# A fused Nystrom attention and SiLU feed-forward kernel: another start for batch 0, exp(C) written straight, a last block in halves, and a new plan

## The chip, the core and the metric

The kernel runs on one core of a Trainium2 chip. The metric is the time of one execution on the device, in microseconds (us). The kernel before takes 275.34 us, the median of three runs (274.78 to 275.83). One further execution was recorded by the profiler; its own time and span are in the table below.

The core's engines appear in the profile under these names: PE (TensorE, matrix products; PEld is its weight load, which overlaps), DVE (VectorE), ACT (ScalarE), POOL (GpSimd) and SP (SyncE, which here only issues DMAs). POOL issues the loads from memory, SP the stores.

## The reference

There are 8 batches of 8 heads, 576 positions and a head size of 64. q, k and v are float32. Each batch goes through an attention with 32 landmarks, and the result through a feed-forward layer of 512 to 2048 to 512 with SiLU between.

```python
q_lm = q.reshape(B, H, 32, 18, D).mean(axis=3)      # landmarks: means of 18 positions
k_lm = k.reshape(B, H, 32, 18, D).mean(axis=3)
A  = softmax(q    @ k_lm.T / 8)                     # 576 x 32
Bm = softmax(q_lm @ k_lm.T / 8)                     # 32 x 32
C  = softmax(q_lm @ k.T    / 8)                     # 32 x 576
Z  = Bm.T / (norm1(Bm) * norminf(Bm) + 1e-6)
for _ in range(6):
    Z = 2 * Z - Z @ Bm @ Z                          # pseudo-inverse of Bm
x = A @ Z @ C @ v                                   # heads side by side: (8*576) x 512
out = silu(x @ w_in) @ w_out                        # 512 -> 2048 -> 512, float32
```

## The kernel before, in words

**What each batch does.** k and q of a batch are loaded by two DMAs each, one to partitions 0 to 63 and one to 64 to 127, and are cast from float32 to bf16 by the loading DMA (`load`). v is loaded by one DMA to 96 partitions, also cast. `landmarks` sums groups of 18 positions: for batches 0 to 2 by products with the identity on PE, for later batches by a tree of additions on POOL in the buffers `treek` and `treeq`; the results `lm` are transposed into `lmT` by DVE. `turn` transposes k and q into `kT` and `qT` on DVE. `scores_b`, `scores_c` and `scores_a` multiply the landmarks with each other, with k and with q.

`exps_c` makes exp(B) (for batch 0 into `be`) and exp(C), which it writes as `pc`; `exps_a` makes exp(A) as `ea`, after `top_a` has subtracted the row maximum in `s_sb`. `norm_b` normalises B to `bm` and prepares the first iterate, `gd` or `gx`. `values` transposes `pc` by products with the identity, copies the result to `pt`, and multiplies it with v. The six steps of the pseudo-inverse are `steps` for batches 0 and 1 (products in `gd` and `tc`, copied by ACT and DVE) and `steps_x` for the later ones. `z_of` gives `zt`, which is Z C v of the eight heads. `weights_a` divides `ea` by its row sums (`asum`, `arec`) and transposes it into `at`.

**The feed-forward layer.** It is never computed from x. `mix` multiplies `zt` with w_in, which gives `m`, 32 landmarks of each head by 2048. `layer1` multiplies `at` with `m` and takes SiLU on ACT into `g`. `layer2` multiplies `g` of a pair of batches with w_out, in blocks of 128 rows by 512 columns: 16 products of 512 columns into `o`, a copy by ACT into `ost`, two stores by SP. There are 36 such blocks.

For batch 0, `mix` makes four parts of 512 columns: part 0 goes to the accumulator `h0`, parts 1 to 3 to `o0` and `o1`. Layer 1 of batch 0 can start once part 0 has been copied to `m` by DVE (first half) and ACT (second half).

**What sets the order.** No loop sets the order of the work. Each operation is added to a planner (`_Plan.add`) with its engine, an estimated duration, the buffers that it reads and writes, and a priority. `_Plan.schedule` then runs a list schedule: at each point it takes, for the engine that is free first, the ready operation with the lowest priority value. It models eight loads in flight on POOL, and the blocks of 256 instructions in which PE's program is fetched. The instructions are issued in the order of planned start times; each engine runs its own in that order, and waits at run time by semaphores for what it reads. `SEQ` is the order in which the stages are added, and `SHIFT` a table of corrections to single priorities.

**Products of zeros.** In gaps of PE, the planner puts products of a buffer of zeros, written to `o1` and read by nobody. Before, they are of 512 columns, go into gaps over 1.0 us, and end for good at the first operation with `hold`, batch 0's first product for the scores of A. There are 14: 10 at the start, 2 behind the landmarks of k and 2 behind those of q.

**The start of the program.** POOL issues the two loads of k of batch 0, then the two of q, then makes the identity matrix, then v, the four loads of w_in, k and q of batch 1, and the four loads of w_out with small operations between.

All products go through the helper `mm` (line 231 in the profile), so the profile tells them apart by their tiles.

Of the kernel before, what the change touches and what calls it, by code (L numbers as in the profile page):

```python
# [16 lines left out]
SEQ = ['E0', 'M0', 'S1', 'L0', 'X1', 'K2', 'M1', 'E2', 'L1', 'M2', 'E3', 'L2', 'M3', 'E4', 'L3', 'M4', 'E5', 'L4', 'E6', 'M5', 'L5', 'M6', 'E7', 'L6', 'M7', 'L7']  # L17
# [3 lines left out]
SHIFT = {'DVE gx t 3': 2, 'DVE brec bsum 2': -1, 'DVE qT qn 3': -0.25, 'PE o zt 0': -0.25, 'ACT xp h 0': -2, 'PE t btd 3': 0.75, 'DVE bm t 2': 2, 'POOL treek 3': 0.25, 'DVE rn n 3': 0.5, 'DVE crec csum 1': -0.5, 'POOL ea arec 1': 1, 'DVE amax s 3': -0.5, 'DVE lmT lm 3': -2, 'PE t gx 3': 2, 'DVE crec csum 3': -0.25, 'DVE pt h 2': -0.25}  # L21

XM = 0.15
# [7 lines left out]
class _Plan:  # L31
# [43 lines left out]
    def schedule(self):  # L75
# [4 lines left out]
        dma_free = 0.0  # L80
# [21 lines left out]
        while left:  # L102
# [27 lines left out]
            if n.tab is not None:  # L130
                if n.tab != tab:
                    occ += 1.3
                tab = n.tab
            if e == "PE" and self.filler is not None:
                from_ = max(free[e], released)
                gap = start - from_
                if n.hold:
                    self.filler = None
                elif gap > 1.0:
                    k = int((gap - 0.3) / 0.35)  # L140
                    for x in range(k):
                        f = _Node()
                        f.start, f.fn = from_ + 0.35 * x, self.filler
# [57 lines left out]
def kernel(  # L201
# [43 lines left out]
    tree = {t: sb(f"tree{t}", [128, 2, 9, D], FP) for t in "qk"}  # L245
# [61 lines left out]
    def emit_consts():  # L307
        V.memset(zero, 0.0)
# [8 lines left out]
        V.memset(tiny, 0.0)  # L317
# [13 lines left out]
    def constants():  # L331
        P.add("DVE", 1.5, emit_consts, w=["mask", "xp", "zero", "tiny", "t0"], prio=-10)
        P.add("POOL", 0.5, emit_ident, w=["s0"], prio=-5)
        P.add("DVE", 0.7, emit_cast, r=["s0"], w=["ident", "two"], prio=-9)
        P.filler = lambda: mm(o_ps[1], zero[:, 0:128], zero)
# [24 lines left out]
    def load(t, src, b):  # L360
        if t == "v":
            def f():
                G.dma_start(  # L363
                    out=nat[t][b % 2][0:96].rearrange("p h j d -> p h (j d)"),
                    in_=src[b].rearrange("h (p j) d -> p h (j d)", j=6))
            P.add("POOL", 0.7, f, w=[f"{t}n{b % 2}"], dma=[2.8],
# [9 lines left out]
        P.add("POOL", 1.4, f, w=[f"{t}n{b % 2}"], dma=[1.4, 1.4], prio=-5 if b == 0 else -0.5)  # L376


    HALF = ((0, 8), (8, SEG))

    def landmarks(b):
        p2 = b % 2
        for ti, t in ((1, "k"), (0, "q")):
# [3 lines left out]
            else:  # L387
                acc, key = t_ps[1][:, 128 * ti:128 * ti + 128], "t1"
# [588 lines left out]
    for x in loads[0:2]:  # L977
        load(*x)
# [96 lines left out]
```

## Time and profile before

| | |
|---|---|
| median of 3 runs | 275.34 us (274.78 to 275.83) |
| profiled execution, its own time | 276.15 us |
| its span | 274.2 us |
| PE busy | 250.6 us, 91% |
| DVE, ACT, POOL busy | 160.6, 169.2 and 121.1 us |
| mean granted PE clock | 0.981 of full speed |
| moved by DMAs | 28.21 MB: 18.35 by POOL's queue, 9.44 by SP's |

The span is the time from the first to the last thing in the record; the execution's own time is 1.95 us longer. Busy time of PE counts overlapped products with ends that are modelled, so a busy PE need not be at its peak rate. "idle before, releaser" at the end of a group's line is the time for which the engine stood idle ahead of these instructions, and what ended it. Bytes of loads that cast are counted as they are written, in bf16.

The order on each engine is known before a run, since the planner writes it out. For the kernel before, PE's order has 14 products of zeros and then batch 0's whole chain up to `mix`; on POOL, k and q of batch 2 are issued behind v of batch 1.

### The profile page before, as it was taken

Reading aid. Unit: us, or ns where it says so; the run is one execution under the profiler, and the core shown is the slowest. Engines: PE = TensorE matmul, PEld = TensorE weight load, DVE = VectorE, ACT = ScalarE, POOL = GpSimd, SP = SyncE. Lnnn points to the kernel's source line nnn. Section 1 sums busy time; section 2 is a strip of 40 time slices with the busy share of each in tenths; the row PEclk is TensorE's granted clock in tenths of the full one; section 3 lists DMA queues with packets and bytes.
Section 4 is the critical chain, followed back from the end, with each engine's and each line's share of the span. In section 5 each row is a group of like instructions: output and inputs, shape, how many; then the busy total and the mean of one; then the engine's idle time right before and its main releaser. Section 6 shows DMA issues by size and latency. Waiting matters only on the chain. (4 is left out here: it accounts for less than half of the span.)

```text
span 274.2 us, 6737 instructions
## 1 busy us (share of the span) xinstructions
PE 250.6 (91%) x2752; PEld 143.6 (52%) x2790; DVE 160.6 (59%) x386; ACT 169.2 (62%) x282; POOL 121.1 (44%) x141
## 2 busy tenths in 40 slices
PE   5764998998899999999999899999999999999992
PEld 1541664733574467445744575546634674654440
DVE  3588848978954994498628974996168733000000
ACT  1187488544875697549755985867728885851111
POOL 8434424699999999743579230430004300000000
PEclk9798699999999999999999999999999999999999
DMA  6999999997595189331962271131013110303333
GB/s 97 202 215 210 206 207 208 210 216 179 90 145 105 39 150 162 66 68 15 202 132 56 54 102 36 41 77 40 14 27 77 43 41 0 78 2 77 77 77 77
DMA packets 19870, 28.21 MB, mean 103 GB/s; under 512 B 1920, under 2 KB 10624, under 8 KB 19840
## 3 DMA queue, kind: packets, MB, share of 16 engines
q0 software_dynamic: 14080, 18.35, 40.0%
q1 hardware_dynamic: 5760, 9.44, 14.9%
q8 instruction: 21, 0.34, 0.5%
q14 instruction: 9, 0.07, 0.1%
HBM read 36.70 MB, written 9.44 MB: 168 GB/s over the span
## 5 line engine op out<-in xcount | busy, mean ns | idle before, releaser
L231 PE MATMUL o<-w_out_sb,g 128*128 128x512 bf16 x539 | 135.3, 379 | 3.8 <-issue 2.4
L231 PEld LDWEIGHTS <-g 128*128 128x128 bf16 x576 | 52.4, 98 | 54.3 <-issue 9.5
L231 PE MATMUL h<-at,m 128*128 128x288 bf16 (+2 forms) x512 | 77.0, 290 | 0.8 <-ACT m L852 0.7
L924 ACT ACTIVATE g<-h 128x576 bf16<-128x576 f32 x112 | 67.5, 651 | 15.8 <-PE h L231 15.7
L231 PEld LDWEIGHTS <-m 128*128 128x128 bf16 x512 | 49.7, 99 | 26.5 <-ACT m L852 1.6
L950 ACT COPY ost<-o 128x512 f32<-128x512 f32 x36 | 21.0, 584 | 47.1 <-PE o L231 43.5
L562 POOL TENSOR_TENSOR s_sb<-s_sb,amax 128x512 f32<-128x512 f32 (+1 forms) x14 | 15.9, 1152 | 38.1 <-DVE amax L556 38.1
L806 DVE CAST m<-h 128x1024 bf16<-128x1024 f32 x14 | 17.1, 1222 | 21.9 <-PE h L231 21.8
L777 DVE SCALAR_TENSOR_TENSOR gx<-gx,t 128x384 bf16<-128x384 bf16 x30 | 16.2, 539 | 13.6 <-PE t L231 13.6
L809 ACT CAST m<-h 128x1024 bf16<-128x1024 f32 x14 | 14.2, 1012 | 12.4 <-PE h L231 12.4
L873 POOL TENSOR_TENSOR ea<-ea,arec 128x640 bf16<-128x640 bf16 (+1 forms) x15 | 17.3, 1165 | 9.1 <-DVE arec L868 9.0
L586 ACT ACTIVATE pc<-h,cneg 128x576 bf16<-128x576 f32 x16 | 18.4, 1216 | 3.6 <-DVE cneg L509 2.4
L689 DVE CAST pt<-h 96x768 bf16<-96x768 f32 x14 | 13.3, 949 | 1.0 <-PE h L231 0.8
L412 POOL TENSOR_TENSOR treeq<-qn 128x1152 f32<-128x1152 bf16 x5 | 11.8, 2364 | 4.1 <-DMA qn<-in_q_dram 4.1
L597 ACT ACTIVATE ea<-s_sb 128x512 bf16<-128x512 f32 (+1 forms) x16 | 12.8, 842 | 1.1 <-POOL s_sb L562 0.7
L363 POOL DMA_DIRECT2D vn<-in_v_dram x8 | 6.5, 813 | 15.6 <-DVE arec L868 8.3
L435 DVE STREAM_TRANSPOSE kT<-kn 128x576 f32<-128x576 f32 x16 | 11.8, 750 | 2.3 <-DMA kn<-in_k_dram 2.3
L907 ACT ACTIVATE g<-h 128x512 bf16<-128x512 f32 (+1 forms) x16 | 9.8, 649 | 5.0 <-PE h L231 4.9
L412 POOL TENSOR_TENSOR treek<-kn 128x1152 f32<-128x1152 bf16 x5 | 11.8, 2370 | 1.8 <-DMA kn<-in_k_dram 1.7
L442 DVE STREAM_TRANSPOSE qT<-qn 128x576 f32<-128x576 f32 x16 | 11.8, 756 | 1.4 <-DMA qn<-in_q_dram 1.4
L412 POOL TENSOR_TENSOR treek<-treek 128x512 f32<-128x512 f32 (+2 forms) x15 | 12.2, 812 | 0.2
L412 POOL TENSOR_TENSOR treeq<-treeq 128x512 f32<-128x512 f32 (+2 forms) x15 | 12.2, 814 | 0.1
(122 smaller groups left out, 306.7 us busy)
## 6 DMA issues: line engine op xcount, KB each, us to landing
out_dram<-ost SPq DMA_DIRECT2D x72, 128.0 KB, 2.4
kn<-in_k_dram POOLq DMA_DIRECT2D x16, 288.0 KB, 8.3
qn<-in_q_dram POOLq DMA_DIRECT2D x16, 288.0 KB, 7.7
vn<-in_v_dram POOLq DMA_DIRECT2D x8, 576.0 KB, 8.4
w_out_sb<-in_moe_w_out_dram POOLq DMA_DIRECT2D x4, 512.0 KB, 17.1
w_in_sb<-in_moe_w_in_dram POOLq DMA_DIRECT2D x2, 768.0 KB, 15.3
w_in_sb<-in_moe_w_in_dram POOLq DMA_DIRECT2D x2, 256.0 KB, 9.3
```

The costliest lines, as they stand in the source:

```text
L231: nc.tensor.matmul(out=out_ap, lhsT=lhsT, rhs=rhs, start=start, stop=stop, tile_position=tp, skip_group_check=True)
L412: lambda: G.tensor_tensor(out=o, in0=a, in1=c, op=OP.add),
L562: E.tensor_tensor(out=sv, in0=sv, in1=mv.unsqueeze(2).to_broadcast((128, 2 * (i1 - i0), LM)), op=OP.subtract),
L586: act(576, lambda qd=qd: A.activation(out=pc[:, qd].rearrange("p (j c) (l t) -> p j c t l", j=2, t=3), in_=h_ps[qd][:, :, 0:SH].rearrange( ...
L597: act(1.3 * n, lambda i0=i0, i1=i1: A.activation(out=ea[:, i0 // 2:i1 // 2].rearrange("p i a m j -> p i j (a m)"), in_=s_sb[:, i0:i1].rear ...
L689: dve(768, lambda dst=dst, src=src: V.tensor_copy(out=dst, in_=src), r=[f"h{qd}"], w=[f"pt{qd}"], prio=0.2)
L777: dve(2 * (192 - lo), lambda a=a, lo=lo, dst=dst: V.scalar_tensor_tensor(out=dst, in0=gx[a][:, :, lo:192], scalar=2.0, in1=t_ps[0][:, 0:38 ...
L806: dve(1024, lambda: V.tensor_copy(out=dst, in_=h_ps[1]), r=["h1"], w=[f"m{b % 2}.{ci}"], prio=0.1)
L809: act(1024, lambda: A.copy(out=dst, in_=h_ps[0]), r=["h0"], w=[f"m{b % 2}.{ci}"], prio=-1)
L873: lambda ev=ev, p0=p0, p1=p1, E=V if on_dve else G: E.tensor_tensor(out=ev, in0=ev, in1=arec[:, p0:p1].rearrange("p i a j -> p (i a) j").u ...
L924: act(576, lambda dc=dc, hp=hp: A.activation(out=g[:, dc, c0:c0 + S].rearrange("p (a n) -> p a n", a=2), in_=hp[:, :, 0:SH], func=AF.Silu) ...
L950: act(512, lambda: A.copy(out=os_, in_=ob), r=[ok], w=[sk], prio=0.5)
```

## The change

1. **k of batch 0.** `first_k` loads it by SP, as float32, into the buffer of the second `g`, which is free until later. Three casts bring it to bf16: DVE takes positions 0 to 6 (896 elements of each partition) and 12 to 17 (768), ACT 7 to 11 (640). POOL's first load is q of batch 0.
2. **Products of zeros** have 256 columns instead of 512 and go into gaps over 0.7 us. They stop at an operation with `hold=1` (now also batch 0's layer 1) and start again after one with `hold=2` (the last transposition of batch 0's `s_sb`). There are 31: 21 at the start, 3 behind the landmarks of q, and 4 and 3 around `z_of` of batch 0.
3. **exp(C)** is written in the order in which it is read, not permuted. So that the product with v still fits, v is loaded with another order of its rows, by three DMAs to 32 partitions each.
4. **The last block** of layer 2 is made in two halves of 256 columns, each copied and stored by itself; of the last half's two stores one is issued by SP and one by ACT.
5. **Smaller things.** The landmarks of q and k of batches 0 and 1 go to two accumulators, not one; both trees on POOL use one buffer; an exp of two elements stands at the start of ACT.
6. **The plan.** `SEQ`, `SHIFT` and `XM` are others, and with all the above the orders change throughout. In the new order: batch 0's `mix` makes `h0` first and then `o0` and `o1`; on DVE, `zt` of batch 0 comes ahead of the second sum of `ea`, and the second subtraction in `s_sb` ahead of the first sum; batch 2's `bm` comes ahead of the sums of `ea`, not behind the first; 8 products of layer 2 stand ahead of batch 1's scores of C, where there were none; the landmarks of q of batch 2 stand behind 30 products of layer 2 instead of 18; and POOL issues k of batch 3 ahead of q of batch 2.

```diff
+            if n.hold == 2:
+                self.fill, released = True, start + n.occ
             if e == "PE" and self.filler is not None:
                 from_ = max(free[e], released)
                 gap = start - from_
                 if n.hold:
-                    self.filler = None
-                elif gap > 1.0:
-                    k = int((gap - 0.3) / 0.35)
+                    self.fill = False
+                if self.fill and gap > 0.7:
+                    k = int((gap - 0.2) / 0.22)
...
-        P.filler = lambda: mm(o_ps[1], zero[:, 0:128], zero)
+        P.filler = lambda: mm(o_ps[1][:, 0:256], zero[:, 0:128], zero[:, 0:256])
...
-                G.dma_start(
-                    out=nat[t][b % 2][0:96].rearrange("p h j d -> p h (j d)"),
-                    in_=src[b].rearrange("h (p j) d -> p h (j d)", j=6))
-            P.add("POOL", 0.7, f, w=[f"{t}n{b % 2}"], dma=[2.8],
+                for t3 in range(3):
+                    G.dma_start(
+                        out=nat[t][b % 2][32 * t3:32 * t3 + 32].rearrange(
+                            "p h j d -> p h (j d)"),
+                        in_=src[b].rearrange("h (l t j) d -> t l h (j d)",
+                                             t=3, j=6)[t3])
+            P.add("POOL", 2.0, f, w=[f"{t}n{b % 2}"], dma=[0.95] * 3,
...
+    def first_k():
+        st = g_sb[1].rearrange("p a n -> p (a n)").bitcast(FP)[
+            :, 0:2 * SEG * D].rearrange("p (a i d) -> p a i d", a=2, d=D)
+        rows = k[0].rearrange("h (l i) d -> (h l) (i d)", i=SEG).rearrange(
+            "(c p) n -> p c n", p=64)
+        flat = st.rearrange("p a i d -> p a (i d)")
+
+        def f():
+            nc.sync.dma_start(out=flat[0:64], in_=rows[:, 0:4:3])
+            nc.sync.dma_start(out=flat[64:128], in_=rows[:, 1:3])
+        P.add("SP", 1.25, f, w=["kst"], prio=-5, lat=4.0)
+        for j, (i0, i1) in enumerate(((0, 7), (7, 12), (12, SEG))):
+            src, dst = st[:, :, i0:i1], nat["k"][0][:, :, i0:i1]
+            n = 2 * D * (i1 - i0)
+            if j == 1:
+                act(n, lambda src=src, dst=dst: A.copy(out=dst, in_=src),
+                    r=["kst"], w=[f"kn0.{j}"], prio=-3)
+            else:
+                dve(n, lambda src=src, dst=dst: V.tensor_copy(out=dst, in_=src),
+                    0.55, r=["kst"], w=[f"kn0.{j}"], prio=-3)
...
-                out=pc[:, qd].rearrange("p (j c) (l t) -> p j c t l", j=2, t=3),
-                in_=h_ps[qd][:, :, 0:SH].rearrange("p j (c t l) -> p j c t l", c=3, t=3), func=AF.Exp, bias=cneg[:, qd:qd + 1],
+                out=pc[:, qd].rearrange("p (j c) n -> p j (c n)", j=2),
+                in_=h_ps[qd][:, :, 0:SH], func=AF.Exp, bias=cneg[:, qd:qd + 1],
...
+        last = pr == B // 2 - 1 and ti == 8
+        n = DM // 2 if last else DM
+        for c0 in range(0, DM, n):
...
+                if c0:
+                    P.add("SP", 0.7, lambda store=store, i0=i0: store(nc.sync, i0, i0 + 1),
+                          r=rk, w=[], lat=2.5)
+                    P.add("ACT", 0.7, lambda store=store, i0=i0, i1=i1: store(
+                        A, i0 + 1, i1), r=rk, w=[], lat=2.5)
...
-    for x in loads[0:2]:
-        load(*x)
+    first_k()
+    load(*loads[1])
```

More of the change, by code (lines that the diff above doesn't have):

```diff
@@ L244 @@
     kT = sb("kT", [128, 2, 6, 3, LM, 2], BF)
-    tree = {t: sb(f"tree{t}", [128, 2, 9, D], FP) for t in "qk"}
+    tree = sb("tree", [128, 2, 9, D], FP)
     lm = [sb(f"lm{i}", [128, 2, 2, D], BF) for i in range(2)]
@@ L956, in f, with store @@
                 ov = out[(2 * pr + x) * S:(2 * pr + x + 1) * S, :].rearrange(
                     "(l i o) f -> i l o f", i=IP, o=2)
[L958 to L961 removed]
+                def store(q, i0, i1, x=x, c_lo=c_lo, p_lo=p_lo, c0=c0, ov=ov):
+                    for i in range(i0, i1):
+                        po = p_lo + 64 * i - c_lo
+                        q.dma_start(out=ov[i, :, :, c0:c0 + n],
+                                    in_=os_[po:po + 64, c0:c0 + n])
```

82 lines of the change are left out of this document (45 added, 37 removed).

## The prediction

> **What bounds the kernel now.** I read the page first (busy time, slices, costliest groups), then windows of 1 us over the start, the timeline of 0 to 56 us, the waits, and the end of the span.
>
> ```profile
> span 274.2 us, 6737 instructions
> PE 250.6 (91%) x2752; PEld 143.6 (52%) x2790; DVE 160.6 (59%) x386; ACT 169.2 (62%) x282; POOL 121.1 (44%) x141
> ...
> PEclk9798699999999999999999999999999999999999
> ...
> GB/s 97 202 215 210 206 207 208 210 216 179 90 145 105 39 150 162 66 68 15 202 132 56 54 102 36 41 77 40 14 27 77 43 41 0 78 2 77 77 77 77
> ```
>
> PE is the bound from the first layer on: from 27 us to its last matmul at 269.2 it idles some 8 us in all, and products of layer 2 fill its gaps. So time is to be had in three places only: before batch 0's first layer, where PE mostly waits; wherever its clock is low; and after its last matmul. The GB/s line shows a second limit: loads run flat out, at 202 to 216 GB/s, for the first 60 us.
>
> Windows of 1 us (busy PE, PEld, DVE, ACT, POOL, then granted clock, DMA share, GB/s):
>
> ```profile
> 7.00:8.00 1.00, 0.82 (x14) 0.85 (x15) 0.85 (x2) 0.00 (x0) 1.00 (x3) 0.92 1.12 212
> ...
> 11.00:12.00 1.00, 0.96 (x12) 0.69 (x10) 0.41 (x1) 0.21 (x1) 0.00 (x0) 0.88 1.31 204
> ...
> 24.00:25.00 1.00, 0.27 (x2) 0.10 (x1) 0.97 (x3) 0.98 (x3) 0.74 (x1) 0.95 1.10 207
> 25.00:26.00 1.00, 0.55 (x16) 0.15 (x16) 0.58 (x3) 0.80 (x2) 0.07 (x1) 0.50 1.09 205
> ...
> 31.00:32.00 1.00, 1.00 (x10) 0.74 (x9) 1.00 (x3) 0.60 (x1) 0.00 (x0) 0.64 1.23 206
> ```
>
> Read as a switch between 1.0 and 0.5, these give a fall at 7.84 us, a rise at 11.24, a fall at 24.90 and a rise at 31.72: steps of 3.4, 4 x 3.4 and 2 x 3.4 us. The clock is decided on a grid of 3.4 us. Of 21.5 to 24.9 PE worked about a third, and the clock fell; of 11.3 to 14.7 about half, and it held. Batch 0's first layer starts at half clock.
>
> The chain of batch 0 and one landmark of batch 2, in the timeline:
>
> ```profile
> 7.15 1.44 DVE L435 STREAM_TRANSPOSE kT<-kn 128x576 f32<-128x576 f32 x2 [2.30 <-DMA kn<-in_k_dram]
> 9.97 1.44 DVE L442 STREAM_TRANSPOSE qT<-qn 128x576 f32<-128x576 f32 x2 [1.39 <-DMA qn<-in_q_dram]
> 12.08 0.31 DVE L422 STREAM_TRANSPOSE lmT<-lm 128x128 f32<-128x128 f32 x1 [0.68 <-ACT lm L404]
> 25.12 0.28 DVE L799 TENSOR_SCALAR zt<-t 128x128 bf16<-128x128 f32 x1
> 27.21 1.89 PE L231 MATMUL h<-at,m 128*128 128x256 bf16 x8 [0.71 <-ACT m L852]
> 49.66 0.50 PE L231 MATMUL h<-qn,ident 128*128 128x128 bf16 x6
> ```
>
> k lands at 7.15, q at 9.97; lmT, from which all scores follow, at 12.08; Z at 25.12; layer 1 at 27.21.
>
> **The change, part by part.** Sums are against the profiled execution, 276.15 us with a span of 274.2; the median of the runs is 275.34, 0.81 lower, and I carry differences over to it.
>
> *k by SyncE, cast.* k now issues at about 0.9 us, when SP is free, not at 1.31 on POOL; q takes POOL's first place, 1.36 earlier. No row shows a load on SP. A store there lands 2.4 us after issue, for 128 KB, or 0.6 us of transfer at 219 GB/s (0.36 of share carries 79 GB/s at 250 to 260): 1.8 us fixed. k is 1.18 MB as float32. At the 410 GB/s that casting loads read (205 written, half the width) it takes 2.9 us and lands at 5.6; at the stores' 219 GB/s 5.4 us, landing at 8.1. I take 6.6, nearer to the loads' row, since q shares the engines. The casts are new: DVE pieces of 896 and 768 elements, ACT one of 640 beside them. The DVE cast of 128 elements took 0.23; at the 1.04 ns an element of its 1024 and 512 casts (1222 and 687) the two take 1.9 us, at half of that 1.1. DVE then still has kT and qT, 2.88 us, ahead of lmT: lmT at 6.6 + 1.1 + 2.88 = 10.6, with slow casts 11.4. PE's landmarks need 2 x 1.0 us at full clock (0.056 each) and 2 x 1.9 at half; with k at 7.7 that ends at 9.8 or 11.5, then 0.3 of copy. The zeros end near 5.2 as before (21 of 256 columns against 10 of 512), so half clock is likely here: lmT at 11.5, a gain of **0.6** (ends: -0.8, k at 8.1 with slow casts; 1.5, all early).
>
> *exp(C) straight.* The 16 pc activations take 1216 ns writing permuted; silu over the same 576 elements, written straight, takes 651: 0.56 less each. In batch 0 the two run from 14.89 to 17.2 ahead of pt, scores and ACT's copies. gd's first product ends near 17.0 whatever pc does, so of 1.1 only about 0.5 comes through, by pt on DVE (17.32) starting earlier. The new DVE order puts the second subtraction ahead of the sum of ea (0.68) and zt ahead of the second sum: zt had been ready at 24.6 and waited for that sum (24.42 to 25.20), 0.5. Together **1.05** (ends 0 and 1.6).
>
> *First layer's start.* mix now makes h0 first, then o0 and o1. Before, mix to layer 1 was 25.45 to 27.21, 1.76 us: h0 came 0.4 later, at half clock. With h0 first: product 0.4, ACT's copy 0.58, 0.1 of hand-over. **0.7** (ends 0, when the clock still falls, and 1.1).
>
> *Zeros up to the first layer.* Seven products of 256 columns, 0.11 us each, go around the last step and z: 0.76 us more activity, into gaps (1.12 and 0.83) in which PE waited anyway, so nothing on the path. With about 1.1 of 3.4 us before, that makes near half of a grid step, what held the clock at 11.3 to 14.7. If it holds, the 4.5 us of layer 1 up to 31.72 shrink by half: **2.3** (ends 0 and 2.6).
>
> The Trainium skill, "TensorE: Matmul & The Clock Gate", Part 1, says that the gate drops to half after an idle window of about 3.4 us. The trace agrees on the window's length, not on "idle": the step that ended at 24.90 had products at 21.66, 22.84 and 24.34. By the page a few products would hold the clock and the 2.3 be sure; by the rows it takes near half a step, and the 2.3 stay uncertain.
>
> *What is late next.* These four make 4.65. But loads stay at 208 GB/s, and the new order of POOL puts batch 3's k ahead of batch 2's q. Nine loads of 0.59 MB and two of 2.1 MB end with that q: 9.5 MB / 208 GB/s = 45.7 us, from about 2.7 (before, the flow reached 205 at 4.2), plus 1 to land: 49.4. Its landmarks stand in PE's order behind products that, by the rates of the chain of work (122 ns for 288 columns, 215 for 512), make 34.3 us of work; at 49.66 PE had done 30.3. So PE can be 4.0 to 4.2 ahead there, no more: of 4.65 I keep **4.1**. w_in, whose last part landed at 24.13 (POOL's wait for it ended there), lands near 22.6 with the earlier flow; mix's second part would ask for it near 23.9, so it hides with 1.3 us in hand.
>
> *Steady stretch.* PE waited for pc 2.1 us in 6 places, 1.0 of it in batches 0 and 1, and 1.08 for bm at 67.58, which stood on DVE behind the sum of ea:
>
> ```profile
> L586 ACT ACTIVATE pc<-h,cneg 128x576 bf16<-128x576 f32 x16 | 18.4, 1216 | 3.6 <-DVE cneg L509 2.4
> ...
> PE h L231 <- ACT pc L586: 2.1, 6, 0.6
> ...
> PE t L231 <- DVE bm L611: 1.9, 2, 1.1
> L363 POOL DMA_DIRECT2D vn<-in_v_dram x8 | 6.5, 813 | 15.6 <-DVE arec L868 8.3
> ```
>
> The order now takes bm first: 2.1 to be had. Against it, v in three issues costs POOL 3 x 0.60 (k's and q's second issue) - 0.81 = 1.0 each time, and POOL is busy 58 of 60 us from 50 to 110; queued behind those issues are ea's products and the landmark sums of later batches, which run far ahead. Their cover could go: DVE waited for them 2.1 us already. One tree buffer for k and q costs nothing, both being on POOL in order. I take **1.0** (ends -1 and 2.1).
>
> *The end.*
>
> ```profile
> 269.24 0.58 ACT L950 COPY ost<-o 128x512 f32<-128x512 f32 x1 [1.57 <-PE o L231]
> ...
> L960 SPq DMA_DIRECT2D out_dram<-ost x72: 533/580/657, 56.5 to 270.4; - x72
> ...
> DMA to landing us min/median/max: 2.3/2.4/7.9
> ```
>
> The last copy is of 256 columns, 0.37 for 0.58; its two stores issue on SP and ACT at once instead of one 0.58 behind the other; they carry 128 KB, not 256, at most 0.3 less. **0.8** (ends 0.2 and 1.0).
>
> Sum: 4.1 + 1.0 + 0.8 = 5.9 us: a profiled span near 268.3, and 275.34 - 5.9 = 269.4.
>
> **The rivals.**
>
> *The clock falls all the same.* For it: the step before 24.90 needs about half, the grid does not move with the chain, and seven zeros reach that only just. Against: the chain runs earlier, so mix and layer 1 reach into the step. Then 2.3 and 0.4 of the 0.7 go, 0.5 of which the late q had taken already: 271.6.
>
> *k lands late.* For it: stores of float32 run at 219 GB/s. k at 8.1 and all loads behind it 2.5 us later put batch 2's q at 51.9, 2.5 later, where 0.5 of the 4.65 was in hand: 2.0 of the 4.1 go, 271.4. Against it: q alone needs the engines from about 3 us on. The Trainium skill, "SBUF — State Buffer", Door 1, says that DMA bandwidth depends on how many of the 16 ports the partitions reach, and a half of k (64 partitions) reaches 8, 217 GB/s by its arithmetic. By that rule this rival is the outcome; that casting loads to 64 partitions write 205 as those to 96 or 128 do bears on neither.
>
> *v in thirds loads at half rate (slower than before).* Each third reaches 32 partitions, for which no row exists; the rows from 64 to 128 partitions show no difference, which speaks against. At half rate v0 and v1 take 2.85 us more each: batch 2's q lands at 55.1, PE is 1.6 behind instead of 4.1 ahead, and v2 takes 1.5 more while loads are still the limit: 4.1 - 5.7 - 1.5 + 1.8 = -1.3, so 276.6. It decides from about 1.9 us a load on.
>
> *The flow starts well and pc is worth all of it.* For it: SP is idle until 56 us; against: nothing shows a load's start there. k at 5.6 moves the cap by 1, waits for pc and bm go whole: 267.
>
> **How the numbers follow.** Forecast 0.45 (its own range 267.5 to 271), clock 0.16, k late 0.14, v in thirds 0.16, better 0.09. A run of this kernel tells some 0.5%, 1.4 us, from no change. Faster by more: nearly all of forecast and better, four fifths of clock and k late: 0.78; within it 0.08; slower 0.14, out of the thirds. The range 266.8 to 274.0 leaves out the thirds and the lower edge of the better case.
>
> **What would show it.** Right: kn cast near 7, lmT below 12, zt near 23.5, layer 1 near 24.7 at clock 1.0 and no 0.5 after 12 us; pc at about 650 ns; batch 2's q landmarks near 49.5; 4.2 us from the last matmul to the end. Wrong: a clock of 0.5 past 20 us, k after 8, loads below 200 GB/s before 50 us, or PE waiting on POOL's landmarks after 60.

## The result, and the profile after

The changed kernel takes 278.81 us (median of 6 runs, 277.39 to 282.4) against 275.58 us for the kernel before on the same chip (6 runs, 274.67 to 276.18). The ratio is 1.0105, with a 95% interval of 1.007 to 1.0141: about 1% slower. Forecast were 269.4 us, and the range ended at 274.0. One of the six runs, that of 282.4 us, was in a slower state of the chip, and the ratio leaves it out. The profiled execution took 278.57 us and has a span of 276.9.

The first page of the profile after, with the lines that answer to those of before (span, busy times, the slices of PE, its clock and the memory rate):

```profile
span 276.9 us, 6870 instructions
...
PE 252.8 (91%) x2823; PEld 147.8 (53%) x2823; DVE 163.0 (59%) x388; ACT 165.3 (60%) x285; POOL 129.2 (47%) x155
...
PE   6178699889789999999999999999999999999994
...
PEclk9567999999999999999999999999999999999999
...
GB/s 133 206 212 210 207 205 203 173 179 188 125 152 119 40 78 144 181 11 76 87 185 84 62 97 66 37 41 58 20 40 60 60 41 0 40 38 52 75 78 100
```

The second slice (6.9 to 13.8 us) has PE at a tenth: it waits for k. From 48 to 83 us four of five slices are below nine tenths. The clock is low at the start, but not at the first layer as it was before.

The timeline of the start (start, duration, engine, line, operation, and in brackets the idle time ahead of it and what ended that):

```profile
0.81 0.74 SPq L396 DMA_DIRECT2D g<-in_k_dram  x1
...
1.61 0.62 SPq L397 DMA_DIRECT2D g<-in_k_dram  x1
...
8.87 0.62 POOL L348 DMA_DIRECT2D w_in_sb<-in_moe_w_in_dram  x1 [2.02 <-DMA qn<-in_q_dram]
12.42 0.72 ACT L403 CAST kn<-g 128x640 bf16<-128x640 f32 x1 [10.12 <-DMA g<-in_k_dram]
12.44 1.09 DVE L406 CAST kn<-g 128x896 bf16<-128x896 f32 x2 [8.76 <-DMA g<-in_k_dram]
12.87 0.78 POOL L381 DMA_DIRECT2D kn<-in_k_dram  x1 [3.38 <-DMA qn<-in_q_dram]
...
17.45 0.31 DVE L455 STREAM_TRANSPOSE lmT<-lm 128x128 f32<-128x128 f32 x1 [1.06 <-ACT lm L438]
```

SP issues k at 0.81 and 1.61, yet it lands at 12.42. POOL's two waits for q, which is loaded in two parts, end at 8.87 and at 12.87: the one part lands ahead of k's end, the other about together with it. Before, k landed at 7.15 and lmT began at 12.08; now lmT begins at 17.45.

Later in the changed kernel's timeline comes a thing that the kernel before does not have, five lines of DVE, POOL and PE around batch 1's chain:

```profile
52.96 2.75 DVE L728 TENSOR_TENSOR crn<-crec,rn 128x2 f32<-128x2 f32 x1
...
53.29 2.40 POOL L445 TENSOR_TENSOR tree<-kn 128x1152 f32<-128x1152 bf16 x1
...
55.63 0.67 DVE L898 TENSOR_REDUCE asum<-ea 128x16 f32<-128x512 bf16 x1
...
56.23 0.40 DVE L779 SCALAR_TENSOR_TENSOR gd<-gd,t 128x256 bf16<-128x256 bf16 x1
...
56.69 0.29 PE L233 MATMUL t<-gd 128*128 128x128 bf16 x2 [2.31 <-DVE gd L779]
```

crn is a product of two numbers a partition; batch 0's took 0.15 us. This one takes 2.75 and ends at 55.71, 0.02 after POOL's sum of the tree. A sum of ea and then gd stand behind it on DVE, and PE waits 2.31 us for gd.

The two profiled executions, cut at events that both have (starts; the table load is ACT's for exp, ahead of batch 1's softmaxes):

| stretch | before | after | difference |
|---|---|---|---|
| start to lmT | 12.08 | 17.45 | +5.37 |
| lmT to layer 1 of batch 0 | 15.13 | 15.11 | -0.02 |
| layer 1 to table load | 14.74 | 14.37 | -0.37 |
| table load to the last copy | 227.29 | 225.97 | -1.32 |
| last copy to the end | 4.96 | 4.00 | -0.96 |
| span | 274.2 | 276.9 | +2.7 |

In the third stretch the changed kernel also does seven products of layer 2, 1.8 us of PE's busy time, that came later before. So that stretch gained 2.2 us, and the fourth, with 1.8 us less to do, lost 0.5, with a wait of 2.31 (shown above) in it.

### The profile page after: what moved, and what is told of

Read it like the earlier page. It is cut to its first block, busy times and chain, and to the rows that moved or that the text cites. A ratio compares the mean times of both kernels' runs of the same rounds, so it can differ in the third digit from the quotient of the medians.

```text
span 276.9 us, 6870 instructions
## 1 busy us (share of the span) xinstructions
PE 252.8 (91%) x2823; PEld 147.8 (53%) x2823; DVE 163.0 (59%) x388; ACT 165.3 (60%) x285; POOL 129.2 (47%) x155
## 3 DMA queue, kind: packets, MB, share of 16 engines
q1 hardware_dynamic: 6128, 10.56, 16.6%
## 4 chain that ended last, share of the span: by engine, by line
PE 72%; DVE 11%; DMA 6%; POOL 5%; ACT 2%; issue 2%; SPq 0%; POOLq 0%; DVEq 0%; ACTq 0%
PE o L233 39%; PE h L233 27%; PE t L233 6%; DMA g<-in_k_dram 4%; POOL tree L445 4%; DMA kn<-in_k_dram 3%; DVE pt L723 2%; DVE cmax L539 1%; DVE asum L898 1%; DVE crn L728 1%; POOL ea L907 1%; ACT g L941 1%; DVE amax L590 1%; ACT L958 0%; DVE s_sb L579 0%
## 5 line engine op out<-in xcount | busy, mean ns | idle before, releaser
L233 PE MATMUL o<-w_out_sb,g 128*128 128x512 bf16 (+1 forms) x592 | 142.4, 374 | 0.0
L233 PE MATMUL h<-at,m 128*128 128x288 bf16 (+2 forms) x512 | 75.6, 286 | 2.5 <-ACT m L886 1.3
L989 ACT COPY ost<-o 128x512 f32<-128x512 f32 (+1 forms) x37 | 21.2, 574 | 43.0 <-PE o L233 41.9
L445 POOL TENSOR_TENSOR tree<-tree 128x512 f32<-128x512 f32 (+2 forms) x30 | 24.7, 822 | 1.8
L368 POOL DMA_DIRECT2D vn<-in_v_dram x24 | 14.2, 599 | 8.0 <-PE t L233 5.6
L620 ACT ACTIVATE pc<-h,cneg 128x576 bf16<-128x576 f32 x16 | 11.7, 734 | 6.5 <-DVE cneg L542 6.3
L445 POOL TENSOR_TENSOR tree<-kn 128x1152 f32<-128x1152 bf16 x5 | 11.9, 2375 | 7.3 <-DMA kn<-in_k_dram 7.2
L539 DVE TENSOR_REDUCE cmax<-h 128x1 f32<-128x576 f32 x16 | 11.4, 750 | 2.8 <-PE h L233 2.7
L233 PEld LDWEIGHTS <-ident 128*128 128x128 bf16 x108 | 8.3, 113 | 7.9 <-issue 7.8
L445 POOL TENSOR_TENSOR tree<-qn 128x1152 f32<-128x1152 bf16 x5 | 11.9, 2371 | 0.4
```

Source lines behind the costliest of these rows:

```text
L233: nc.tensor.matmul(out=out_ap, lhsT=lhsT, rhs=rhs, start=start, stop=stop, tile_position=tp, skip_group_check=True)
L368: G.dma_start(out=nat[t][b % 2][32 * t3:32 * t3 + 32].rearrange("p h j d -> p h (j d)"), in_=src[b].rearrange("h (l t j) d -> t l h (j d)" ...
L445: lambda: G.tensor_tensor(out=o, in0=a, in1=c, op=OP.add),
L539: dve(576, lambda qd=qd: V.tensor_reduce(out=cmax[:, qd:qd + 1], in_=h_ps[qd][:, :, 0:SH], axis=AX.XY, op=OP.max), r=[f"h{qd}"], w=[f"cmax ...
L989: act(n, lambda ob=ob, c0=c0: A.copy(out=os_[:, c0:c0 + n], in_=ob[:, 0:n]), r=[ok], w=[sk] if c0 == 0 else [sk + "b"], prio=0.5)
```

## The experiments

Ratios are to the kernel before, run beside each kernel on the same chip. My theory after the result: k's load on SP is the loss, and the other parts bring about what they were meant to. The rivals: another part costs as well, or the parts bring nothing.

### How k comes: five ways

k back on POOL as a casting load ahead of q, all else as changed:

```
-        dma_free = 4.0
+        dma_free = 0.0
...
-    first_k()
-    load(*loads[1])
+    for x in loads[0:2]:
+        load(*x)
```

> The changed kernel with one part undone: batch 0's k is again the first load of POOL, cast by the load, with no casts on DVE and ACT; the planner writes a new order from that. Theory 1 (k's late landing, 12.4 us against 7.15, is the whole loss, and the other parts gain as forecast): k lands near 7.2, lmT near 12, zt near 24, layer 1 near 26, no clock of 0.5 after 12 us, and a time of 270 to 272. Theory 2 (the other parts, the new order above all, lose by themselves): lmT near 12 all the same, but a time of 275 or more.

Measured: 273.23 us (10 runs, 271.47 to 274.99), ratio 0.9912 [0.9881, 0.9943]. kT began at 7.38, lmT at 12.60, layer 1 at 27.33. Theory 1 holds in the main, and theory 2 does not. But Z (25.04) and layer 1 came some 1 us later than it said, the clock fell to half once more behind 12 us (16.6 to 20.0), and the time is poorer than its 270 to 272. Without part 1 the change is 0.9% faster, and part 1 makes the 5.6 us between 273.23 and 278.81, the whole loss and more.

The opposite, the kernel before with only k's new way (`first_k` and the casts as shown with the change, left out here):

```
-    for x in loads[0:2]:
-        load(*x)
+    first_k()
+    load(*loads[1])
```

> The kernel before with that one part alone: k of batch 0 by SP as float32, with the three casts, POOL's loads starting with q. Theory 1: k lands past 11, lmT past 16, and since the rest of the kernel before has nothing to win the delay back, the time is some 4 to 5 us above that of before, 279 to 281. Theory 2: within 1.5 us of before.

Measured: 282.43 us (4 runs), ratio 1.0237 [1.0183, 1.0291], even above the 279 to 281 of theory 1. Its casts began at 12.38 on DVE; ACT's waited until 13.65, since without the change's early exp its table load (1.28) stood in front; lmT began at 18.52.

What makes k late? Three versions of the changed kernel. First, POOL's loads held until k has landed (every load after this gate waits for it):

```
...
+    def hold_loads():
+        P.gate = P.add("POOL", 0.1, lambda: G.tensor_copy(
+            out=held, in_=P_st[0][:, :, SEG - 1, D - 1]), r=["kst"], w=["held"], prio=-8)
...
     first_k()
+    hold_loads()
     load(*loads[1])
```

> The changed kernel with POOL's loads held back: POOL reads one element of k's float32 buffer before its first load, so q and all that follow are issued only after k has landed. Sharing (k is late because POOL's queue takes about half of the DMA engines' time): k lands at 5.5 to 6.5 if it then moves at the 410 GB/s of the casting loads, at about 8 if it moves at the 219 GB/s of the float32 stores, in both cases far ahead of 12.4. SP's queue slow by itself: k still past 11. q lands some 6 us after k in any case, so the time is no measure here.

Second, the same with q let go at once, v and w_in held (the edit against the first):

```
     first_k()
-    hold_loads()
     load(*loads[1])
+    hold_loads()
```

> The changed kernel, with SyncE's float32 k beside batch 0's q alone: POOL issues v, w_in and all later loads only once k has landed. k landed at 12.42 us beside everything and at 9.27 with nothing beside it. Theory 1 (whatever is under way shares the engines, and q is the first to take them): q alone takes its 0.59 MB / 208 GB/s = 2.8 us from k, k lands at 11.5 to 12.2 and q near 9. Theory 2 (v and w_in behind q are what k loses to): k lands at 9.3 to 10.2. The time is no better than the changed kernel's either way (278 to 281 us), since what is held lands later.

Third, the float32 load and the casts kept, but issued by POOL, first in the queue that q, v and w_in stand in:

```
-            nc.sync.dma_start(out=flat[0:64], in_=rows[:, 0:4:3])
-            nc.sync.dma_start(out=flat[64:128], in_=rows[:, 1:3])
+            G.dma_start(out=flat[0:64], in_=rows[:, 0:4:3])
+            G.dma_start(out=flat[64:128], in_=rows[:, 1:3])
...
```

> The changed kernel with k still as float32 into the same buffer and cast by DVE and ACT, but issued by POOL as its first two loads, ahead of q in one queue. Sharing: k lands at 7 to 8, q near 10 to 11, since one queue serves in order. Width (writing float32 is what is slow): k at 9 or later, q at 12 or later. Against the run with the casting load the difference of k's landing is the price of the width alone.

One execution each. The lines of the three timelines, in that order, that show k's landing (the cast that waited for it):

```profile
9.27 0.73 ACT L414 CAST kn<-g 128x640 bf16<-128x640 f32 x1 [6.96 <-DMA g<-in_k_dram]
```

```profile
11.97 0.72 ACT L414 CAST kn<-g 128x640 bf16<-128x640 f32 x1 [9.66 <-DMA g<-in_k_dram]
```

```profile
9.78 0.72 ACT L403 CAST kn<-g 128x640 bf16<-128x640 f32 x1 [7.48 <-DMA g<-in_k_dram]
```

| k's load | lands |
|---|---|
| casting, POOL, first in the queue | 7.38 |
| float32, POOL, first in the queue | 9.78 |
| float32, SP, nothing beside it | 9.27 |
| float32, SP, q beside it | 11.97 |
| float32, SP, q, v and w_in beside it (changed kernel) | 12.42 |

So the 5.0 us from 7.38 to 12.42 are two things. The width: some 2 us, whichever engine issues. The windows of 2 us of the version with nothing beside k:

```profile
4.00:6.00 2.00, 1.26 (x10) 0.89 (x8) 0.00 (x0) 0.00 (x0) 0.00 (x0) 1.00 1.06 242
6.00:8.00 2.00, 0.00 (x0) 0.00 (x0) 0.00 (x0) 0.00 (x0) 0.00 (x0) 0.95 0.92 194
```

The last number of a line is the rate in GB/s: 218 GB/s in the mean, with nobody else there, so k at full width goes at the stores' rate. The Trainium skill, "SBUF — State Buffer", Door 1, gives about 218 GB/s as the limit of a transfer to 64 partitions, and 196 as measured at 1 MiB; this run's mean agrees with the limit, though one of its two windows is above it. And the sharing: q beside it costs 2.70 (9.27 to 11.97), just the 2.8 us that q's 0.59 MB take at 208 GB/s, and v and w_in 0.45 more. In the changed kernel the DMA view of 4 to 6 us shows both queues under way, q1 SP's and q0 POOL's (packets, MB, share of the 16 engines' time):

```profile
q1 hardware_dynamic: 91, 0.35, 65.8%
q0 software_dynamic: 55, 0.13, 33.3%
```

that of 8 to 10 us about as many packets of the one as of the other:

```profile
q1 hardware_dynamic: 64, 0.29, 71.6%
q0 software_dynamic: 61, 0.14, 37.3%
```

and that of 10 to 12 us POOL's ahead, while k's last pieces are still out:

```profile
q0 software_dynamic: 337, 0.30, 94.7%
q1 hardware_dynamic: 34, 0.08, 26.8%
```

A second queue brought no second bandwidth. In the slice of 6.9 to 13.8 us the page shows 206 GB/s, for 202 before. What it did was to take away k's turn ahead of the others. The Trainium skill, "DMA: Bandwidth & Descriptors", Queues, rings and completion order, says that each DMA engine takes the queues in turn, a packet of each; the 64 and 61 packets of 8 to 10 us agree.

The times of the two held versions (280.07 and 282.18, one run each) are no better than the changed kernel's, as expected, since what is held lands later; the second is above its range. The version with float32 on POOL took 273.31 in its one run, as much as the casting load, though k came 2.4 us later. That is one execution, and what it says of k's worth is weak.

### The other parts one at a time

The kernel before with only the last block in halves (all of the diff's part in `layer2`, of which this is the core):

```
+        last = pr == B // 2 - 1 and ti == 8
+        n = DM // 2 if last else DM
+        for c0 in range(0, DM, n):
...
+                if c0:
+                    P.add("SP", 0.7, lambda store=store, i0=i0: store(nc.sync, i0, i0 + 1),
+                          r=rk, w=[], lat=2.5)
+                    P.add("ACT", 0.7, lambda store=store, i0=i0, i1=i1: store(
+                        A, i0 + 1, i1), r=rk, w=[], lat=2.5)
```

> The kernel before, with only the last block in halves and its last two stores on two queues. Theory (the end is a part of its own, worth the 0.96 us by which the stretch from the last copy to the span's end shrank, 4.96 to 4.0): 0.8 to 1.0 us faster than before, 274.6 to 274.8 us, and nothing changes ahead of the last block. Rival (the stores' fixed time ends the span either way, and the copy was hidden by it): within 0.3 us of before.

Measured: 275.6 us against 275.45 (10 and 25 runs), ratio 0.9994 [0.997, 1.0017]. Nothing is shown to be gained, though a gain up to 0.8 us isn't excluded. The end of its timeline tells why:

```profile
267.05 0.86 ACT L955 COPY ost<-o 128x512 f32<-128x512 f32 x2 [2.90 <-PE o L231]
...
267.68 1.91 PE L231 MATMUL o<-w_out_sb,g 128*128 128x256 bf16 x16 [0.28 <-ACT ost L955]
...
269.62 0.37 ACT L955 COPY ost<-o 128x256 f32<-128x256 f32 x1 [1.72 <-PE o L231]
```

The last copy starts at 269.62 (before 269.24): the second half's products waited 0.28 us for ACT to have copied the buffer that they write. From there to the end it is 4.58 us, for 4.96 before and 4.00 in the changed kernel. What the smaller end gave, the buffer took.

The kernel before with only exp(C) straight and v in thirds:

```
-                out=pc[:, qd].rearrange("p (j c) (l t) -> p j c t l", j=2, t=3),
-                in_=h_ps[qd][:, :, 0:SH].rearrange("p j (c t l) -> p j c t l", c=3, t=3), func=AF.Exp, bias=cneg[:, qd:qd + 1],
+                out=pc[:, qd].rearrange("p (j c) n -> p j (c n)", j=2),
+                in_=h_ps[qd][:, :, 0:SH], func=AF.Exp, bias=cneg[:, qd:qd + 1],
```

> The kernel before, with only exp(C) written straight and v loaded in thirds; the planner orders the rest anew only where this moves it (PE's order differs in some 240 lines). Forecast's step: pc 1.22 to 0.73 us, 0.5 us off batch 0's chain and some of the 2.1 us that PE waits for pc: 0.5 to 1.5 us faster, 274.1 to 275.1 us, Z earlier than 25.1 us. Rival (the chain waits for something else beside pc, and POOL pays three issues for one): Z at 25.0 to 25.3 us, 275.3 to 276.5 us. Thirds at half rate would show as v0 landing 2.8 us later.

Measured: 274.86 us against 275.45 (10 and 25 runs), ratio 0.9978 [0.9951, 1.0006]: 0.6 us, which is in the range expected of the step but not clear of noise. In its profile lmT to Z took 12.35 us for 13.04, and layer 1 began at 26.43 for 27.21. v in thirds did no harm here: POOL's wait for batch 0's v ended at 13.09 for 13.08.

The version with k on POOL, with the products of zeros as before (their width of 512 columns and their spacing are left out here):

```
-                    self.fill = False
-                if self.fill and gap > 0.7:
-                    k = int((gap - 0.2) / 0.22)
+                    self.filler = None
+                elif gap > 1.0:
+                    k = int((gap - 0.3) / 0.35)
```

> The version with k on POOL (273.2 us), with the products of zeros as before: 512 columns, in gaps over 1 us, none after the scores. Forecast's step (zeros up to the first layer hold the clock there, 2.3 us): the granted clock falls to 0.5 ahead of the first layer and stays there until about 31.7 us, 274.5 to 276.5 us. Rival (the stretch from the first layer to ACT's table load is set by ACT's and DVE's copies, not by PE's clock; it was 14.7 us at half clock and 14.4 at full): 273.0 to 273.8 us even if the clock falls.

Measured: 274.54 us (10 runs, 272.19 to 276.21), ratio 0.9957 [0.9921, 0.9993]; with the zeros it was 0.9912 [0.9881, 0.9943], so the zeros are worth 1.2 us with an uncertainty of about the same size. The mechanism is plain in the windows. Without them:

```profile
28.00:30.00 2.00, 2.00 (x19) 1.14 (x17) 0.26 (x1) 0.85 (x2) 1.84 (x4) 0.50 1.22 206
```

and with them (columns as in the windows of before, the clock third from the end):

```profile
28.00:30.00 2.00, 1.94 (x27) 1.51 (x25) 1.35 (x2) 1.32 (x3) 2.00 (x3) 1.00 1.22 205
```

Layer 1 to the table load is 16.03 us without, 14.37 with, and one product of layer 2 fewer is done. In these two profiles the rival (copies set that stretch, whatever the clock) falls. This version's profile also has the stall of crn (2.73 us at 48.64), so its time isn't the zeros' alone.

The version with k on POOL, with the three settings of the old plan (SEQ, SHIFT, XM):

> The version with k on POOL (273.2 us), planned with the three settings of the kernel before (SEQ, SHIFT, XM). Theory 1 (the gains of the parts add up: 2.4 us in all, of which some 0.6 was exp(C) straight, some 1.2 the zeros, 0 the end, so 0.6 is left for the plan): 273.6 to 274.2 us. Theory 2 (the new plan costs: from 64 to 74 us PE sat idle 3.5 us, waited 1.5 us for g behind a table load and fell to half clock for 3.4 us): 271.8 to 272.9 us.

Measured: 280.58 us (4 runs), ratio 1.0162 [1.0089, 1.0235]. Neither theory had that. The waits of PE by what ended them (us in total, times, the longest) show three long ones that were not there:

```profile
PE h L233 <- DVE pt L723: 3.5, 2, 3.0
...
PE t L233 <- DVE bm L645: 2.7, 1, 2.7
...
PE t L233 <- DVE gx L752: 2.5, 1, 2.5
```

The clock, too, fell to half for 3.4 us three times behind 70 us (at 72.8, 127.4 and 164.9), where k on POOL has one such fall. The parts don't add up one by one: settings that fit one set of durations put other durations in a bad order.

### More zeros at the start

With k on POOL the clock still fell from 16.6 to 20.0 us (granted 0.65 in the window of 16 to 18, 0.50 in 18 to 20, 1.00 in 20 to 22), behind a stretch (14 to 16) with 0.47 us of products. Zeros into columns that the scores leave free can run there:

```
-                if self.fill and gap > 0.7:
-                    k = int((gap - 0.2) / 0.22)
+                if self.fill and gap > (0.3 if start > 11 else 0.7):
+                    k = int((gap - 0.1) / 0.13 if start > 11 else (gap - 0.2) / 0.165)
...
-        P.filler = lambda: mm(o_ps[1][:, 0:256], zero[:, 0:128], zero[:, 0:256])
+        P.filler = lambda: mm(o_ps[1][:, 320:512], zero[:, 0:128], zero[:, 0:192])
...
-                   prio=(0.3, 1.2)[b], margin=0.2, hold=1, ni=32)
+                   prio=(0.3, 1.2)[b], margin=0.2, ni=32)
```

> The version with k on POOL (273.2 us), with products of zeros of 192 columns that also run between the scores and the first step (14.0 to 15.6 us, where PE had 0.47 us of work in 2) and more of them around the steps. Theory (PE's idle time there made the clock fall from 17.3 to 20.7 us, and the eight products of a step took twice as long): no 0.5 after 12 us, Z at 24.2 to 24.7 us for 25.04, 272.2 to 272.8 us. Rival (the steps wait for ACT's and DVE's copies between them): the clock holds, Z is at most 0.2 us earlier, 273.0 to 273.5 us.

Measured: ratio 0.9886 [0.9808, 0.9964] (272.93 us, 4 runs, on a chip where the kernel before took 276.34). The expectation puts the fall 0.7 us too late; the windows give 16.6. Now the clock was 1.0 from 12 us on, Z came at 23.93 for 25.04, layer 1 at 26.18 for 27.33: more than the theory asked. But the time is the same within its interval. The gain is given back at batch 2's q, as the timeline of 51 us shows:

```profile
51.26 0.51 PE L233 MATMUL h<-qn,ident 128*128 128x128 bf16 x6 [1.23 <-DMA qn<-in_q_dram]
```

With k on POOL and the fewer zeros the same products began at 51.31, with no wait: first layers 1.15 us apart, the same moment here.

### The stall of crn

The changed kernel, with crn as two products with a scalar operand in place of one with two tensor operands:

```
-            dve(1, lambda: V.tensor_tensor(out=crn, in0=crec, in1=rn, op=OP.mult),
+            dve(1, lambda: [V.tensor_scalar(out=crn[:, x:x + 1], in0=crec[:, x:x + 1], scalar1=rn[:, x:x + 1], scalar2=None, op0=OP.mult) for x in range(2)],
```

> The changed kernel (278.8 us), with crn, two numbers a partition, as two products with a scalar operand and no second tensor operand; all else and every order the same. In the changed kernel crn took 2.75 us at 53 us, until POOL's sum of 1152 elements beside it ended, and PE then waited 2.3 us. Theory (VectorE's operation with two tensors in SBUF waits for POOL's that reads SBUF): crn takes 0.13 us each, PE's wait of 2.3 goes, 276.3 to 277.0 us. Rival (DVE or its port is held up by POOL whatever crn's form): crn or the operation behind it takes 2.5 us again, 278 to 279.5 us. If PE only waits for the next late thing, crn is short and the time within 0.5 us of the changed kernel's.

Measured: 276.62 us (10 runs, 274.11 to 278.22) against 276.34, ratio 0.9995 [0.9954, 1.0037]. To have the changed kernel on one chip with the next two, it ran again:

> The changed kernel itself, beside the next two on one chip, as the base of their differences (it and the version without crn's wait had been compared through the kernel before, on two chips). 278.5 to 279.3 us if the kernel before is at 275.6; crn at batch 1 again takes 2.5 to 2.8 us until POOL's sum ends.

278.81 us (12 runs) against 275.95, ratio 1.0089 [1.0057, 1.012], with crn at 2.74 us. So the stall costs 0.94% with an uncertainty of 0.5% (two chips, each with the kernel before beside it): 2.6 us, give or take 1.5, most of the net loss. The timeline of the version without it, at the same place:

```profile
53.98 0.33 DVE L728 TENSOR_SCALAR crn<-crec,rn 128x1 f32<-128x1 f32 x2
54.03 0.27 PE L233 MATMUL t<-gd 128*128 128x128 bf16 x2
...
54.29 2.41 POOL L445 TENSOR_TENSOR tree<-kn 128x1152 f32<-128x1152 bf16 x1
...
54.82 0.41 DVE L779 SCALAR_TENSOR_TENSOR gd<-gd,t 128x256 bf16<-128x256 bf16 x1
...
55.29 0.28 PE L233 MATMUL t<-gd 128*128 128x128 bf16 x2
```

POOL's sum runs as before, DVE goes on beside it, and PE's wait of 2.31 is gone.

The same profile shows something about the zeros. They are those of the changed kernel, and yet the clock fell right at the first layer, which began at 31.48, and stayed at half from 29.8 to 36.6 us:

```profile
30.00:32.00 2.00, 0.91 (x11) 0.40 (x4) 2.00 (x5) 0.58 (x1) 0.25 (x1) 0.50 1.23 206
```

Layer 1 to the table load took 16.46 us here, for 14.37 in the changed kernel. The steps of 3.4 us in which the clock is decided lie elsewhere in each execution: one begins at 28.78 us in the changed kernel's profile, and here at 26.40. In the step ahead of this fall PE was busy for 1.76 us. In the step that ended just ahead of the first layer, and behind which the clock held, it was 1.91 in the changed kernel and 2.04 with k on POOL. So the zeros seem to bring PE only just to what holds the clock, and whether it holds in one execution is partly luck. Where the edge lies isn't settled: with nothing beside k, 1.66 us were once enough, far from the first layer.

The same edit with k on POOL, where the profile had shown no such stall (crn came at 47.73, 0.9 us ahead of POOL's sum):

> The version with k on POOL and with crn as two products with a scalar operand. If crn's wait and the late k are two causes that add up (5.6 us between the changed kernel and k on POOL, 2.9 of it crn): the collision is absent with k on POOL already (its profile had crn at 0.15 us, 0.9 us ahead of POOL's sum), so nothing is gained on 273.2 us: 272.8 to 273.6. If it happens there too in some executions (they range from 271.5 to 275.0 us): 272.0 to 272.8 us, with a narrower spread.

Measured: 273.93 us (7 runs), ratio 0.9925 [0.9891, 0.9959], the 0.9912 of k on POOL within the intervals. Nothing is gained where there is no stall, so in the changed kernel the two causes are linked: there the late k brings batch 1's chain to where crn meets POOL's sum. Of the 5.6 us that part 1 costs, about half is that meeting, with the same uncertainty of 1.5. A late k is not the whole condition, though. In the two versions that hold loads back, lmT was as late (17.53 and 17.00) and crn took 0.16; with k on POOL and the old zeros k was early and crn took 2.73. What decides is where the orders of the two engines bring these two operations together.

### A version that beats both

k on POOL, more zeros, crn as scalar products:

> The same, with the products of zeros between the scores and the first step as well: the fastest version that these runs point to. Without crn's product of two tensors it should stay at 272.2 to 272.9 us (1.0 to 1.3 per cent below before). What it gains at the start (Z 1.5 us earlier) it loses where PE waits for batch 2's q near 51 us, unless that lands earlier.

Measured: 273.31 us (6 runs) against 275.95, ratio 0.9902 [0.9868, 0.9936]. Its landmarks of batch 2's q begin at 51.29, after a wait of 1.14. It beats both kernels, no more than k on POOL alone does. The new plan loads batch 3's k ahead of that q; one edit turns this round:

```
-              dma=[1.4, 1.4], prio=-5 if b == 0 else -0.5)
+              dma=[1.4, 1.4], prio=-5 if b == 0 else -0.5, after=[P.last_w["qn0"]] if (t, b) == ("k", 3) else ())
```

> The version with k on POOL, more zeros and crn as scalar products (0.9902 of the kernel before), with batch 3's k loaded behind batch 2's q instead of ahead of it. Forecast's cap (the landing of batch 2's q limits what the start may gain; it was at 51.3 us in four versions whose first layer began anywhere from 26.2 to 27.3): q lands near 48.5 us, PE's wait of 1.1 us goes, its landmarks run from about 50 us: 0.9855 to 0.989 of before, 271.9 to 272.9 us. Rival (1.1 us is taken up by the next late thing, PE's wait for silu behind ACT's table load near 70 us): the landmarks run earlier and the time stays at 0.989 to 0.992.

Measured: 274.88 us (12 runs), ratio 0.9972 [0.9943, 1.0], slower than without it and outside both ranges. The landmarks began at 49.62 with no wait, as the cap says. The planner, with the loads moved, ordered what follows anew, and PE waited elsewhere:

```profile
67.67 0.19 PE L233 MATMUL t<-eps,mask 128*128 128x64 bf16 x1 [2.44 <-DVE bm L645]
```

But the two profiles, with and without this edit, part earlier than that: at ACT's table load this version is 2.16 us behind (42.77 for 40.61). Of that, 0.9 is there at lmT (12.77 for 11.90), and 1.3 comes in the first layer, where this execution's clock was at half from 26.8 to 30.2 us in spite of the zeros, and the other's was not. From the table load to the last copy it is even a little quicker, 227.20 for 227.81, with the wait above in it. So q's landing does hold PE up at 51 us, and removing that alone did not pay; why not stays open, since one profile with a fall of the clock can't tell for twelve runs. Whether another order would pay wasn't tried.

## Why the prediction was wrong, step by step

**The step that failed: k by SyncE, cast.** "I take 6.6, nearer to the loads' row, since q shares the engines." k landed at 12.42, beyond both ends (5.6 and 8.1). Two errors. The width: the upper end, 8.1, had the right rate, 219 GB/s, and k alone landed at 9.27. The sharing: I put q first in POOL's queue and counted it as a reason for the early end; but its bytes go beside k's, and k ends later by all of them. 8.1 and q's 2.8 us would have made 10.9 from rows that the prediction had; measured, 9.27 and 2.70 make 11.97 (why k alone took 1.2 longer than 8.1 isn't shown; from 2 to 4 us it moved only 152 GB/s). The casts were right (0.63 and 0.55 us on DVE for 1.1 together), as was the half clock after the idle wait. lmT came 5.37 later where 0.6 earlier was forecast. The rival "k lands late" had the rate but not the sharing, and stopped at 271.4.

**The cost that no step had: DVE beside POOL.** The prediction priced POOL only as a queue. crn's 2.75 us, some 2.6 us of time (give or take 1.5), is in none of its terms.

**exp(C) straight**, 1.05: pc took 0.73 for 1.22, 0.48 saved where 0.56 was taken. In the changed kernel lmT to Z is 0.2 us shorter (13.04 to 12.82), with the clock low from 22 to 25 us; with that mended by more zeros it is 11.92 with k on POOL, 1.1 shorter. With exp(C) straight alone it was 12.35, 0.7 shorter. The size was right for this part and the new order of DVE together, if the clock is held.

**First layer's start**, 0.7: nothing. Z to layer 1 is 2.09 before and 2.29 after. Before, layer 1 began (27.21) behind one copy of h, ACT's, while DVE's had just started. Now h came first, but ACT was still loading its table (29.85 to 31.13); DVE copied first (31.20 to 31.88), ACT's copy waited for it (31.91), and layer 1 came behind both. I had counted one copy.

**Zeros up to the first layer**, 2.3: right in size where the clock held. Layer 1 to the table load, net of layer 2's products, gained 2.2, at a clock of 1.0; taking them away with k on POOL gave 1.7 us back in that stretch. But two later profiles with zeros, that without crn's stall and the last one, have the clock at half in the first layer all the same. The rival "the clock falls all the same" named this; it took the grid to stay where it was, and the grid lies elsewhere in each execution.

**What is late next**, the cap by batch 2's q: right as a mechanism. Its landmarks begin at 51.3, not at 49.4, in four versions with k on POOL whose first layers began from 26.2 to 27.3, three of them after a wait for it. Why they came 1.9 us after the forecast moment isn't shown. In the changed kernel, with everything late, it cost nothing.

**Steady stretch**, 1.0: not shown. In the profile of k on POOL, table load to last copy is 225.57 for 227.29, and the 1.8 us of layer 2's products done earlier are as much as that difference.

**The end**, 0.8: 0.96 in the changed kernel, between -0.5 and 0.8 by itself.

The rival on the slower side, v in thirds at half rate, is not what happened: v did no harm. The sign came from part 1, so the 0.14 that was given to a slower kernel rested on a cause that isn't the one.

## What to carry to other kernels

A transfer on a second queue is not beside the first: add the bytes of whatever is under way ahead of the critical load, at the rate measured, and in the width in which they are written (here 205 GB/s of bf16 with a cast, 218 of float32 without). A change ahead of a chain also moves the chain against the other engines, so look in the trace for small operations that would stand where POOL's long ones run; a two-number product can cost what a big one does. Filling gaps to hold the clock is not safe when it only just reaches what holds it. And where a planner lays out the work, an edit's worth alone isn't its worth among the others: undo parts in the final kernel, as well as do them alone in the first.

## What was not expected of the hardware

DVE's product of two small tensors in SBUF waited out POOL's operation: it ended 0.02 us after POOL's in the changed kernel (2.75 us), in its second profile (2.74) and with the old zeros (2.73), each time beside the sum of 1152 elements. With k's new way alone it took 0.79 us, beside POOL's product of ea:

```profile
55.12 1.04 POOL L902 TENSOR_TENSOR ea<-ea,arec 128x512 bf16<-128x512 bf16 x1 [3.33 <-DVE arec L897]
...
55.39 0.79 DVE L723 TENSOR_TENSOR crn<-crec,rn 128x2 f32<-128x2 f32 x1
```

Both end at 56.2. In the form with a scalar operand it took 0.2 us, with POOL's sum starting 0.02 us before the end of the second, so that no run shows this form in the midst of the sum; and gd's product, with one operand in PSUM, took 0.41 beside that sum, as it did without it. The Trainium skill, "SBUF — State Buffer", Who interferes with whom, says that a VectorE operation with two inputs in SBUF and a GpSimd operation that reads SBUF use a port pair that one of them holds to its end; these rows agree. By the page's rule the one that starts first has it. In the changed kernel DVE's start is shown 0.33 us ahead of POOL's, and DVE lost; POOL had been issuing a load (52.67 to 53.29) when DVE's product came, and its sum followed at once. The starts on POOL are rough in the profile, so that is not settled here.
